# Turning queries and keys: six tokens in a row on each partition, two tokens per product, in all of the early attentions

## The chip, the cores and the metric

The kernel runs on one core of one Trainium2 chip. The metric is the time of one execution on the device in microseconds (us). Three runs of the kernel before took 796.45, 794.44 and 797.93 us; their median is 796.45 us.

## What is computed

Four batches of eight heads, 768 tokens, 64 numbers per head. Attention is local (tokens less than 16 apart) plus one summary per block of 32 tokens: the block's largest key in each coordinate and its mean value. The heads side by side then form a 768 x 512 matrix per batch, which goes through a two-dimensional Fourier mix, a normalisation and a two-layer network. In short:

```
k_sum = k.reshape(B, H, nb, 32, D).max(axis=3);  v_sum = v.reshape(B, H, nb, 32, D).mean(axis=3)
scores = concat(where(|i-j| < 16, q k^T / 8, -1e9), q k_sum^T / 8 + log(32))
x = softmax(scores) @ concat(v, v_sum)          # heads side by side: (4, 768, 512)
u = x + real(fft over tokens of fft over columns of x)
out = u + relu(norm(u) @ w_ch1) @ w_ch2
```

All arithmetic is in float32; the weights arrive as 64-bit floats and are converted on the chip.

## The kernel before

The heads are worked in pairs: pair g holds heads 2g (e = 0) and 2g + 1 (e = 1), whose 64 coordinates fill 128 partitions. For the scores, queries and keys have to stand with the coordinates on the partitions and the tokens along the row (tiles `qt` and `kt`, 128 x 768). In memory they stand the other way, so each pair is loaded with tokens on partitions (`load`) and turned (`prepare`).

There are three ways of turning. Batch 0 (`is_wide`) loads three tokens in a row on each partition (768 bytes), half h of the tokens at a time. For every half, each of the three tokens and each of the two heads, TensorE multiplies the 128 x 64 block by the identity (line 718) and writes the result three columns apart into a bank of PSUM; the bank then stands in token order for both heads, and ScalarE copies it (128 x 384, line 719) into a contiguous piece of `kt` or `qt`. A tensor takes twelve such products and two copies. Batch 1, and pair 0 of batch 2, load two tokens in a row (512 bytes, three pieces j for each head) and turn the 128 x 128 block of both tokens in one product (line 725): six products a tensor. One product's result has the first token on partitions 0 to 63 and the second on 64 to 127, so four copies of 64 x 384 (line 727) write the columns two apart. All later pairs go through a transposition on VectorE (line 711); the change doesn't touch them.

The first attention (`first_attention`, batch 0) is laid down in the order of the program on TensorE and VectorE: nothing is moved there by a scheduler. For each pair: the scores of one half (line 748, products in which the two heads alternate; line 752, the scores of the block summaries, which need the key maxima of line 700), the exponentials on ScalarE (line 754), the multiplication by the mask on VectorE (line 571); then the second half; then `finish_pair` for the pair before (values, line 775), then `prepare` of the pair after next, then `sum_values` (line 765 on TensorE, line 767 as a copy). Pairs 0 and 1 are prepared ahead of this loop and within its first step. When the pairs are done, the Fourier mix of batch 0 starts (lines 1252 and 1256, with copies at 1257 and 1258), and the attention of batch 1 is woven in between by a driver that deals out steps; there line 791 are the scores, 814 and 816 the block sums and their scaling, 826 and 831 the values.

All loads named here go out on SP's queue, in program order while the first part runs. The PSUM banks of the turning come from a pool of four (`bank` in batch 0, `abank` later; in the latter the scores and the values of attention stand too). ScalarE takes its instructions in order, so copies, exponentials and conversions of weights (lines 1091 and 1104) queue behind each other.

Of the kernel before, what the change touches and what calls it, by code (L numbers as in the profile page):

```python
# [16 lines left out]
P = 128  # L17
# [471 lines left out]
def _main_program(ctx, tc, q, k, v, moe_w_ch1, moe_w_ch2, out):  # L489


    nc = tc.nc
    B, H, S, D = q.shape
    DM = H * D
    DF = moe_w_ch1.shape[1]
    NST = S // P
# [7 lines left out]
    S2 = S // 2  # L504
    F2 = S // 4
    HT = NST // 2
# [17 lines left out]
    ident = cpool.tile([P, P], FP, name="ident")  # L524
# [24 lines left out]
    def fetch(out, in_):  # L549

        ins = nc.sync.dma_start(out=out, in_=in_)
        if in_order[0]:
            tc.keep_in_program_order(ins)
        return ins.ins

    def abank(shape, name):
        return psum.tile(shape, FP, tag="attn", bufs=4, name=name)

    def bank(shape, name):
        return psum.tile(shape, FP, tag="bank", bufs=4, name=name)  # L560
# [16 lines left out]
    nat, marks = {}, {}  # L577

    def load(b, g, *which):

        for n in which or (1, 0):
            t = nat[b, g, n] = apool.tile([P, 2, NST // 2, 2 * D], FP, tag="nat", bufs=4, name=f"{'qk'[n]}n_{b}_{g}")
            if (b, g) > (2, 0):
                t = nat[b, g, n] = t.rearrange("p e j n -> p (e j n)").rearrange("p (m c) -> p m c", c=32)
                for e in range(2):
                    for h in range(2):
                        r, o = D * e + 32 * h, (q, k)[n][b, 2 * g + e].offset + 32 * h
                        fetch(out=t[r:r + 32], in_=bass.AP((q, k)[n].tensor, o, [[D, 32], [32 * D, S // 32], [1, 32]]))
                continue
            if is_wide(b):  # L590
                t = nat[b, g, n] = t.rearrange("p e j n -> p (e j n)").rearrange("p (e h s d) -> p e h s d", e=2, h=2, s=HT)
                fetch(out=t.rearrange("p e h s d -> p (e h) (s d)"),
                      in_=(q, k)[n][b, 2 * g:2 * g + 2].rearrange("e (h p s) d -> p (e h) (s d)", p=P, s=HT))
                continue
            fetch(out=t.rearrange("p e j n -> p (e j) n"),
                  in_=(q, k)[n][b, 2 * g:2 * g + 2].rearrange("e (j p s) d -> p (e j) (s d)", p=P, s=2))

# [59 lines left out]
    is_wide = lambda b: b == 0  # L659
# [39 lines left out]
    def key_maxima(g):  # L699
        nc.vector.tensor_reduce(out=km_bufs[g % 2][:, 0:nb], in_=kt_bufs[g % 2][:, W:W + S].rearrange("p (n f) -> p n f", f=BLOCK),  # L700
                                op=ALU.max, axis=AX.X)

    def prepare(b, g, *which):
        qn, kn = (nat[b, g, n] for n in range(2))
        kt = kt_bufs[g % 2]
        qt = apool.tile([P, S], FP, tag="qt", name=f"qt_{b}_{g}") if 0 in (which or (0,)) else None
        for n in which or (1, 0):
            src, dst = (kn, kt[:, W:W + S]) if n else (qn, qt)
            if (b, g) > (2, 0):
                with tc.issue_after(marks["dense"]):  # L710
                    nc.vector.transpose(out=dst, in_=src.rearrange("p m c -> p (m c)"))
                continue
            if is_wide(b):
                for h in range(2):
                    ps = bank([P, S2], f"qk_{b}_{g}_{h}")
                    for s in range(HT):
                        for e in range(2):
                            nc.tensor.matmul(ps[D * e:D * (e + 1), s:S2:HT], src[:, e, h, s, :], ident, start=True, stop=True)
                    nc.scalar.copy(out=dst[:, S2 * h:S2 * (h + 1)], in_=ps)
            else:  # L720
                for e in range(2):

                    ps = abank([P, S2], f"qk_{b}_{g}_{e}")
                    for j in range(NST // 2):
                        nc.tensor.transpose(ps[:, P * j:P * (j + 1)], src[:, e, j, :], ident)
                    for s in range(2):
                        nc.scalar.copy(out=dst[D * e:D * (e + 1), s:S:2], in_=ps[D * s:D * (s + 1)])  # L727
        if which == (0,):
            nat[b, g] = qt
            return  # L730
        if (b, g) != (1, 1):
            with tc.issue_after(marks["fold", 0]) if (b, g) == (1, 0) else ExitStack():
                key_maxima(g)
        nat[b, g] = qt
# [113 lines left out]
    def first_attention():  # L848
# [3 lines left out]
        wt["fold"] = split_fold(0, fold)  # L852
        p = {0: wide_scores(0, 0, lambda: add_blocks(0))}
        prepare(0, 1)
        sum_values(0, 0)
        load(0, 3)
        def finish_pair(g):
            wide_values(0, g, p[g], x)
# [9 lines left out]
        for g in range(NP - 1):  # L868
            p[g + 1] = wide_scores(0, g + 1, (None, lambda: add_blocks(1), finish_last_but_one)[g])
            if g < NP - 2:  # L870
                finish_pair(g)
                prepare(0, g + 2)
                sum_values(0, g + 1)
                for par in range(2):
                    fold_sequence(par, g)
            if g == NP - 3:
                load(1, 0)
                get_tables(0, lambda: load_raw(1))
                load_raw(2)
                sum_values(0, g + 2)  # L880
# [106 lines left out]
    def gen_attention(b):  # L987
# [3 lines left out]
        if b == 2:  # L991
            load(2, 1)
            load(2, 2)
# [7 lines left out]
        for g in range(NP + 1):  # L1001
# [44 lines left out]
            if n1:  # L1046
                prepare(*n1, *((1,) if b > 1 else ()))
# [432 lines left out]
    ps = bank([P, 512], "warm")  # L1480
# [18 lines left out]
    for vw in vw_bufs:  # L1499
        nc.gpsimd.tensor_copy(out=vw[:, :, D].rearrange("p (e n) -> p e n", e=2),  # L1500
                              in_=count[:, None, :].to_broadcast([P, 2, NQ]))
# [51 lines left out]
    for b in range(B):  # L1553
# [14 lines left out]
        if b == B - 2:  # L1568
# [9 lines left out]
            ps = bank([1, 1], "flag_ps")  # L1578
# [42 lines left out]
```

## Time and profile before

| what | value |
|---|---|
| median of three runs | 796.45 us |
| the profiled execution | 793.7 us |
| its span on the page | 791.9 us |
| granted TensorE clock | 0.999 |
| TensorE busy | 776.3 us, 98% |
| VectorE busy | 492.0 us, 62% |
| ScalarE busy | 224.7 us, 28% |
| turning copies of batch 0 (line 719) | 16 of 128x384, 478 and 479 ns in the mean |
| turning copies of batch 1 and pair (2,0) (line 727) | 40 of 64x384, 507 and 508 ns in the mean |
| first attention | from about 5 us to 44 us of the span |

The page gives busy time by engine and the chain of work that ended last; PEld is TensorE's loading of the stationary operand, which overlaps the products. A timeline shows instructions in order of time, like ones merged; the bracket after a line gives the idle time before it and who ended it.

### The profile page before, as it was taken

To read this page: it belongs to the slowest core of one execution; us is meant where nothing else is said; L and a number is where in the kernel's file an instruction comes from. 1 tells how busy PE (TensorE), PEld (TensorE's weight loads), DVE (VectorE), ACT (ScalarE), POOL (GpSimd) and SP (SyncE) were. 2 spreads that over 40 slices of the span, in tenths; PEclk is the share of its full clock that TensorE was granted. 3 is DMA by queue.
4 is the path that set the end of the run, shared out by engine and by line. 5 is a ranking of instruction groups with operands and counts; after the bars stand their busy time and mean duration, and the time that the engine had idled before them with its cause. 6 is when DMAs were issued, how large, how long until landed. Compare 5 with 4: busy or idle time off the path is not lost.

```text
span 791.9 us, 14352 instructions
## 1 busy us (share of the span) xinstructions
PE 776.3 (98%) x5920; PEld 562.9 (71%) x5920; DVE 492.0 (62%) x1019; ACT 224.7 (28%) x491; POOL 47.9 (6%) x85
## 2 busy tenths in 40 slices
PE   8998999999999999999999999999999999999997
PEld 6777655445588866787578866788569875886686
DVE  5899988787988556752758544653677623533352
ACT  3564757226525022100236012200226111001200
POOL 0000000000000020200210020300120000000000
PEclk9999999999999999999999999999999999999999
DMA  9999787695956179976342169610614153106001
GB/s 212 189 262 246 190 268 190 210 284 201 240 186 152 46 206 263 218 110 184 137 153 94 54 208 211 183 55 11 243 37 140 54 215 134 51 0 233 0 28 56
DMA packets 133353, 121.82 MB, mean 154 GB/s; under 512 B 94464, under 2 KB 114912, under 8 KB 133088
## 3 DMA queue, kind: packets, MB, share of 16 engines
q1 hardware_dynamic: 132160, 118.53, 54.0%
q0 software_dynamic: 576, 2.10, 0.8%
q8 instruction: 48, 0.79, 0.4%
q10 hardware_dynamic: 544, 0.20, 0.1%
q14 instruction: 25, 0.20, 0.1%
HBM read 97.22 MB, written 23.59 MB: 153 GB/s over the span
## 4 chain that ended last, share of the span: by engine, by line
PE 88%; DVE 5%; ACT 4%; DMA 2%; issue 1%; DVEq 0%
PE hx L1368 19%; PE ox L1437 18%; PE hz L1368 9%; PE oz L1437 9%; PE hy L1368 5%; PE o L1414 5%; PE oy L1437 5%; PE y L1252 3%; PE sc L791 2%; PE mx L1211 2%; PE av L826 2%; PE unt L1342 1%; PE av L831 1%; DMA qn<-in_q_dram 1%; PE ss L808 1%; ACT kt L727 1%
## 5 line engine op out<-in xcount | busy, mean ns | idle before, releaser
L1368 PE MATMUL hx<-u,w 128*128 128x384 f32 x512 | 185.4, 491 | 2.4 <-ACT h L1385 1.0
L1368 PEld LDWEIGHTS hx<-u,w 128*128 128x128 f32 x512 | 95.2, 190 | 71.3 <-ACT p L797 3.8
L1368 PE MATMUL hz<-u,w 128*128 128x384 f32 x256 | 93.0, 486 | 0.0
L1437 PE MATMUL oz<-w,s 128*128 128x256 f32 x336 | 81.3, 380 | 0.0
L1437 PE MATMUL ox<-w,s 128*128 128x256 f32 x336 | 80.1, 380 | 0.0
L1437 PE MATMUL ox<-w,h 128*128 128x256 f32 x336 | 79.6, 381 | 0.0
L571 DVE TENSOR_TENSOR x<-ox,x 128x256 f32<-128x256 f32 x84 | 35.5, 422 | 66.2 <-PE ox L1437 65.9
L1368 PEld LDWEIGHTS hz<-u,w 128*128 128x128 f32 x256 | 48.6, 190 | 33.9
L1437 PEld LDWEIGHTS ox<-w,h 128*128 128x128 f32 x336 | 63.1, 190 | 10.8 <-issue 1.2
L1437 PEld LDWEIGHTS ox<-w,s 128*128 128x128 f32 x336 | 63.2, 190 | 9.1 <-DVE x L571 0.3
L1437 PEld LDWEIGHTS oz<-w,s 128*128 128x128 f32 x336 | 63.3, 190 | 8.9 <-DVE x L571 0.4
L1379 ACT COPY h<-hx 128x384 f32<-128x384 f32 x32 | 15.3, 477 | 191.6 <-PE hx L1368 191.5
L571 DVE TENSOR_TENSOR h<-hy,h 128x384 f32<-128x384 f32 x32 | 17.8, 557 | 48.9 <-PE hy L1368 48.8
L1368 PE MATMUL hy<-u,w 128*128 128x384 f32 x128 | 46.8, 487 | 0.0
L571 DVE TENSOR_TENSOR h<-hx,h 128x384 f32<-128x384 f32 x32 | 17.8, 556 | 45.2 <-PE hx L1368 44.0
L1414 PE MATMUL o<-w,h 128*128 128x512 f32 x96 | 42.2, 595 | 0.7 <-DVE w L571 0.7
L1398 ACT ACTIVATE h<-hx 128x384 f32<-128x384 f32 x32 | 15.7, 489 | 89.4 <-PE hx L1368 89.4
L1437 PE MATMUL oy<-w,h 128*128 128x256 f32 x168 | 40.1, 380 | 0.0
L571 DVE TENSOR_TENSOR x<-oz,x 128x256 f32<-128x256 f32 x42 | 17.8, 423 | 30.4 <-PE oz L1437 30.1
L1368 PEld LDWEIGHTS hy<-u,w 128*128 128x128 f32 x128 | 24.2, 190 | 17.1 <-DVE h L571 0.7
L1437 PEld LDWEIGHTS oy<-w,h 128*128 128x128 f32 x168 | 31.8, 190 | 4.4
L1414 PEld LDWEIGHTS o<-w,h 128*128 128x128 f32 x96 | 18.0, 190 | 23.6 <-issue 20.7
(166 smaller groups left out, 1072.5 us busy)
## 6 DMA issues: line engine op xcount, KB each, us to landing
w<-dw SPq DMA_DIRECT2D x44, 896.0 KB, 5.6
words<-in_moe_w_ch_dram SPq DMA_DIRECT2D x32, 512.0 KB, 5.8
dw<-w SPq DMA_DIRECT2D x12, 896.0 KB, 7.0
vw<-in_v_dram SPq DMA_DIRECT2D x47, 192.0 KB, 6.2
out_dram<-x SPq DMA_DIRECT2D x23, 256.0 KB, 2.0
vb<-in_v_dram SPq DMA_DIRECT2D x24, 192.0 KB, 7.2
kn<-in_k_dram SPq DMA_DIRECT2D x9, 384.0 KB, 6.3
qn<-in_q_dram SPq DMA_DIRECT2D x9, 384.0 KB, 6.9
```

Of the source, the lines that this page charges most:

```text
L571: return nc.vector.tensor_tensor(out=out, in0=in0, in1=in1, op=op).ins
L727: nc.scalar.copy(out=dst[D * e:D * (e + 1), s:S:2], in_=ps[D * s:D * (s + 1)])
L791: nc.tensor.matmul(ps[h][r:r + 64, i, :], kt[rows, o:o + 64], qt[rows, o:o + BLOCK], start=True, stop=True)
L808: nc.tensor.matmul(ps[r:r + 32, :], km[rows, :], qt[rows, S2 * h:S2 * (h + 1)], start=True, stop=True)
L826: nc.tensor.matmul(av[r][32 * j:32 * (j + 1), t, :], p[rows, h, i - NB2 * h, :], vw[rows, i, :], start=(t == 0), stop=False, skip_group_ch ...
L1211: nc.tensor.matmul(out, y[:, g], table, start=False, stop=True, skip_group_check=True)
L1252: nc.tensor.matmul(y, fgs[b][par][:, st, P * g:P * (g + 1)], fs[par][:, g % 2, st, :], start=(st == 0), stop=(st == n - 1))
L1368: ins = nc.tensor.matmul(ps, w[:, a, kk, :], u[:, r, kk, :], start=start and kk == 0, stop=stop and kk == 1, skip_group_check=True)
L1379: nc.scalar.copy(out=c11, in_=X)
L1398: nc.scalar.activation(out=c21, in_=X, func=AF.Relu)
L1414: nc.tensor.matmul(ps, h[:, n, hf, P * t:P * (t + 1)], wt[2, b, j][:, 2 * hf:2 * hf + 2, :], start=(n, hf) == (0, 0), stop=(n, hf) == (NC ...
L1437: nc.tensor.matmul(ps, left[a][:, n, :], wt[2, b, j][:, r, :], start=start and n == 0, stop=stop and n == NC - 1, skip_group_check=True)
```

## The change

`load` now takes one form for all pairs up to (2,0): six tokens in a row on each partition, 1536 bytes, 256 rows per tensor. Partition p holds tokens 6p to 6p + 5 of each head. `prepare` turns two of them at once in 128 x 128 products, three products a head, in batch 0 too. Product j gives the tokens 6p + 2j (partitions 0 to 63) and 6p + 2j + 1 (64 to 127) for all p. Four copies per tensor of 64 x 384 put them in token order: for a fixed j they write columns six apart, and the three j lie two columns from each other. The queries of the very first pair are copied by VectorE, all else by ScalarE. The order of the instructions on the engines and queues is otherwise the same.

```
-            if is_wide(b):
-                t = nat[b, g, n] = t.rearrange("p e j n -> p (e j n)").rearrange("p (e h s d) -> p e h s d", e=2, h=2, s=HT)
-                fetch(out=t.rearrange("p e h s d -> p (e h) (s d)"),
-                      in_=(q, k)[n][b, 2 * g:2 * g + 2].rearrange("e (h p s) d -> p (e h) (s d)", p=P, s=HT))
-                continue
-            fetch(out=t.rearrange("p e j n -> p (e j) n"),
-                  in_=(q, k)[n][b, 2 * g:2 * g + 2].rearrange("e (j p s) d -> p (e j) (s d)", p=P, s=2))
+            fetch(out=t.rearrange("p e j n -> p e (j n)"),
+                  in_=(q, k)[n][b, 2 * g:2 * g + 2].rearrange("e (p t) d -> p e (t d)", p=P))
...
-            if is_wide(b):
-                for h in range(2):
-                    ps = bank([P, S2], f"qk_{b}_{g}_{h}")
-                    for s in range(HT):
-                        for e in range(2):
-                            nc.tensor.matmul(ps[D * e:D * (e + 1), s:S2:HT], src[:, e, h, s, :], ident, start=True, stop=True)
-                    nc.scalar.copy(out=dst[:, S2 * h:S2 * (h + 1)], in_=ps)
-            else:
-                for e in range(2):
-
-                    ps = abank([P, S2], f"qk_{b}_{g}_{e}")
-                    for j in range(NST // 2):
-                        nc.tensor.transpose(ps[:, P * j:P * (j + 1)], src[:, e, j, :], ident)
-                    for s in range(2):
-                        nc.scalar.copy(out=dst[D * e:D * (e + 1), s:S:2], in_=ps[D * s:D * (s + 1)])
+            for e in range(2):
+
+                ps = (bank if is_wide(b) else abank)([P, S2], f"qk_{b}_{g}_{e}")
+                for j in range(NST // 2):
+                    nc.tensor.transpose(ps[:, P * j:P * (j + 1)], src[:, e, j, :], ident)
+                for s in range(2):
+                    copy = nc.vector.tensor_copy if (b, g, n) == (0, 0, 0) else nc.scalar.copy
+                    copy(out=dst[D * e:D * (e + 1)].rearrange("r (p j s) -> r j p s", p=P, s=2)[:, :, :, s],
+                         in_=ps[D * s:D * (s + 1)].rearrange("r (j p) -> r j p", p=P))
```

## The prediction

> **What bounds the kernel now.** I read the busy shares first, then the chain that ended last, then the timeline of the first 50 us, then the groups by shape.
>
> ```profile
> PE 776.3 (98%) x5920; PEld 562.9 (71%) x5920; DVE 492.0 (62%) x1019; ACT 224.7 (28%) x491; POOL 47.9 (6%) x85
> ...
> PE 88%; DVE 5%; ACT 4%; DMA 2%; issue 1%; DVEq 0%
> ```
>
> TensorE is busy 98% of the span and owns 88% of the chain. So 1 us in which TensorE has nothing to do is nearly 1 us of time, and ACT's 28% is an average that says nothing of the 30 us where the change sits. The timeline of the third head pair's turning (g = 2 of batch 0; columns: start, us, engine, line, operation, in brackets the idle time before it and who ended it):
>
> ```profile
> 21.59 1.35 PEld L718 LDWEIGHTS qk<-ident,kn 128*64 128x64 f32 x24
> ...
> 22.57 0.48 ACT L719 COPY kt<-qk 128x384 f32<-128x384 f32 x1 [1.39 <-PE qk L718]
> ...
> 22.86 1.40 PEld L718 LDWEIGHTS qk<-ident,qn 128*64 128x64 f32 x24
> ...
> 23.27 0.48 ACT L719 COPY kt<-qk 128x384 f32<-128x384 f32 x1 [0.23 <-PE qk L718]
> ...
> 23.93 1.08 ACT L719 COPY qt<-qk 128x384 f32<-128x384 f32 x2 [0.18 <-PE qk L718]
> ...
> 24.76 1.10 PEld L748 LDWEIGHTS sc<-qt,kt 64*96 64x96 f32 x24
> ```
>
> Products lead here and ACT waits for them. From the first product to the first score it is 24.76 - 21.59 = 3.17 us; keys take 22.86 - 21.59 = 1.27 us of products. The same view gives 30.74 to 34.13 = 3.39 us for pair 3. In pair 1 ACT is held by the exponentials until 12.93, its first key copy starts at 12.88, and scores start at 15.70: 2.82 us. In pair 0 products start at 5.13 and scores at 8.09. Batch 1 already turns two tokens at once; there ACT leads:
>
> ```profile
> 73.30 0.64 PEld L725 LDWEIGHTS qk<-ident,kn 128*128 128x128 f32 x6 [0.62 <-issue]
> ...
> 73.88 2.06 ACT L727 COPY kt<-qk 64x384 f32<-64x384 f32 x4
> 73.90 0.69 PEld L725 LDWEIGHTS qk<-ident,qn 128*128 128x128 f32 x6
> ...
> 75.96 2.11 ACT L727 COPY qt<-qk 64x384 f32<-64x384 f32 x4
> ...
> 77.04 0.82 PEld L826 LDWEIGHTS av<-vw,p 64*32 64x32 f32 x62 [0.44 <-ACT qt L727]
> ...
> 78.65 0.75 PEld L831 LDWEIGHTS av<-vs,p 64*128 64x128 f32 x12 [0.79 <-ACT vs L816]
> ```
>
> A tensor's products take 73.90 - 73.30 = 0.60 us, but its four copies 2.06 us (0.52 us from start to start), and TensorE twice waits on ACT.
>
> **What the Trainium skill says.** "SBUF — State Buffer", section "Door 1: The DMA port swizzle", says SBUF has 16-byte lines, that two hits per line are needed for full speed, and that each access to a new line pays; it names 4 fp32 as the free limit and gives no price. The copies now write fp32 two apart (8 bytes, two per line); the changed ones write six apart (24 bytes, a new line each). The trace of before has one large access of that kind, a DVE reduction reading 64 apart:
>
> ```profile
> L650 DVE TENSOR_REDUCE vbs<-vb 96x64 f32<-96x512 f32 x2 | 2.1, 1026 | 0.0
> ...
> L700 DVE TENSOR_REDUCE km<-kt 128x24 f32<-128x768 f32 x16 | 15.1, 942 | 7.9 <-ACT kt L719 5.8 <-ACT kt L727 2.1
> ```
>
> With 0.15 us fixed (the two-point fit of L700 and the 192-element reduction at L1576, 354 ns), that is (1026-150)/512 = 1.71 ns an element against (942-150)/768 = 1.03: a factor of 1.66. So the trace agrees for reads. No row has strided writes over 8 bytes. Second, "TensorE: Matmul & The Clock Gate", section "What's actually happening", says the clock halves after an idle window of about 3.4 us and comes back after one busy window. The trace before has no such idle stretch (clock 9 in all slices).
>
> **The change part by part.**
>
> *Products, batch 0.* Twelve per tensor become six: 1.27 us becomes 0.60 us. Eight tensors: 8 x 0.67 = 5.4 us of TensorE work removed. It is a gain only where copies don't follow; they do.
>
> *Copies, batch 0.* Two of 128x384 (0.478 us) per tensor become four of 64x384 with a new stride. All tokens are interleaved now, so the scores, which alternate the two heads, need all eight copies of a pair; before they started after the third of four. ACT's price: 512 elements take 583 ns (L1343) and 384 take 478 (L719), so 0.82 ns an element and 0.163 us fixed. Bounds: below, 0.39 us a copy (two exponentials of 128x384 are 0.87 us together, 0.385 apart); the nearest row, L727, says 0.52; above, twice the time an element, 0.163 + 384 x 1.64 = 0.79. (In pairs 2 and 3 the key copies also wait for one another on ACT's own counter, as L727's do; the 0.52 contains that.) I take the factor 1.66: 0.163 + 384 x 1.36 = 0.69, 0.70 from start to start. For DVE: 0.15 + 384 x 1.71 = 0.81, 0.74 apart (its neighbours start some 0.07 before the end of the last).
>
> - Pair 2: the first copy starts after three products, 0.30, and the same tail as now (0.98 - 6 x 0.106 = 0.34): 0.64 + 8 x 0.70 + 0.06 = 6.30, against 3.17: +3.1.
> - Pair 3: 6.30 against 3.39: +2.9.
> - Pair 1: 8 x 0.70 + 0.06 = 5.66 against 2.82: +2.8. Its query transfer, landing at 13.77, is hidden by the key copies.
> - Pair 0: queries go to DVE, beside the keys on ACT. Queries landed at 1.24 + 5.1 = 6.34; longer rows may bring that 0.2 forward (512 packets of 768 bytes at 36 ns are 1.15 us on 16 engines; a 4632-byte row's rate, 181 ns, would make 256 of 1536 bytes 0.96). First copy at 6.14 + 0.64 + 0.07 = 6.85, last ends 3 x 0.74 + 0.81 = 3.03 later: scores at 9.9 instead of 8.09: +1.8. Queued behind the DVE copies is the key maximum (0.95 us), needed only 1.1 us after the scores begin: hidden.
>
> Sum, batch 0: 10.6 us. Nothing in TensorE's hand-written order fills these gaps; the sum products at L765 (0.34 us) lie inside them already. L767 on ACT and the multiplications on DVE shift along. After 45 us TensorE is again without a gap (14.69 of 15 us busy from 45 to 60), so nothing later absorbs the delay.
>
> *Copies, batch 1 and pair (2,0).* The count stays at 40, each dearer by 0.70 - 0.52 = 0.18 us. Pair (1,1), shown above: eight copies stand before L816, for which TensorE waits: +1.4. Pair (1,2), from 84.74 on: products wait for key copies (0.38 and 0.34 us) and L814 for query copies (0.69): +1.4. Pair (1,0), six copies from 46.0, 1.1 us, of which the 0.32 us idle ahead of L1257 takes part: +0.7. The rest stand beside dense products: +0.6. Sum 4.1. If the writes cost nothing, zero.
>
> *Loads.* Half or a third of the packets, same issues in the same order on SP; POOL untouched. TensorE waits 0.4 us in all for q and k, so beyond pair 0 I count nothing; if that cover were gone it would be at most that 0.4. The clock gate: TensorE idles about 4.7 us in each of pairs 2 and 3, enough for a halved window (up to 1.7 us each of three pairs, 5 us); zero taken, kept for the upper end.
>
> Total +14.7 us. The profiled execution took 793.7 us (span 791.9 plus 1.8 around it): 808.4. The median of the runs shown is 796.45, 2.75 above: 811.2.
>
> **The rivals.**
> 1. Strided writes cost nothing (0.52 us a copy, as L727). For it: reads and writes may differ. Pairs: 8 x 0.52 = 4.16, so +1.7, +1.5, +1.4, and +0.8 for pair 0 (DVE 3 x 0.48 + 0.55): +5.4, batch 1 unchanged: 801.9.
> 2. Twice the time an element (0.80 apart): +3.9, +3.7, +3.6, +2.3 = 13.5, batch 1 4.1 x 0.28/0.18 = 6.4, and one clock window 1.7: 818.
> 3. Not slower: two copies overlap like the exponentials, 0.385 apart, on ACT between copies of one bank. Then the shorter products nearly pay for them: +0.6, +0.4, +0.4 for pairs 2, 3 and 1, +0.8 for pair 0 (DVE as in 1), together 2.2, less 0.3 for earlier landings: 798.3, no change that can be told. It decides below 0.47 us from start to start (24 copies x 0.09 above 0.385 would add 2.1). Against it: L727 is 0.52 apart even where no wait stands between.
> That the change isn't made as told is excluded: the built order shows x3 products and eight 64x3x128 copies a pair, four of them on DVE.
>
> **How the numbers follow.** The likeliest, 811.2: 0.47. Rival 1: 0.27. Rival 2: 0.14. Rival 3: 0.09. Something unseen that makes it faster: 0.03. Half a percent, 4.0 us, is about what a measurement of this kernel can tell from no change. Faster 0.03, same 0.12 (rival 3 and a cheap rival 1), slower 0.85. The range reaches from the cheap side of rival 1 to rival 2: 800 to 819.
>
> **What would show it.** Copies of 64x384 near 0.69 us on ACT and 0.8 on DVE; scores of pair 2 some 6.3 us after its first product, TensorE idle before them with ACT as releaser; products 0.60 us a tensor; L816 of pair (1,1) 1.4 us later after its first key copy. Wrong if the copies are at 0.52 or less, if the scores start before the eighth copy, or if TensorE's gap is filled.

## The result, and the profile after

The changed kernel takes 837.78 us (median of 6 runs, 836.47 to 843.85) against 795.67 us before (6 runs, 794.44 to 797.93): 42.1 us slower, a ratio of 1.0535 with a 95% interval from 1.0507 to 1.0564. The forecast had the direction, but not the size: 811.2 us, with 819 as the upper end. The profiled execution took 838.19 us, its span is 836.4 us. (For one kernel below, whose copies write side by side, the ratio leaves out the slowest four of 20 runs, as over 1.5% above its fastest.)

The page of the kernel after, busy shares, the granted clock by slices, and the chain that ended last:

```profile
PE 794.2 (95%) x5776; PEld 573.4 (69%) x5776; DVE 496.7 (59%) x1023; ACT 253.6 (30%) x503; POOL 47.8 (6%) x85
...
PEclk7769979999999999999999999999999999999999
...
PE 84%; ACT 7%; DVE 5%; DMA 2%; issue 1%; POOL 0%; SPq 0%; DVEq 0%; POOLq 0%
```

Two things are new. ACT's share of the chain went from 4% to 7%, roughly 27 us more (7% of 836.4 less 4% of 791.9, both shares rounded). And TensorE is busy for 17.9 us *more* than before although it has fewer instructions (5776 for 5920): the row PEclk, 9 in every slice before, shows 7, 7, 6 in the first three and a 7 in the sixth, of 20.9 us each. TensorE ran slower there.

The timeline of the third pair's turning, the same stretch that the prediction showed of before:

```profile
35.10 0.64 PEld L712 LDWEIGHTS qk<-ident,kn 128*128 128x128 f32 x6
...
35.69 3.40 ACT L715 COPY kt<-qk 64x384 f32<-64x384 f32 x4 [1.65 <-PE qk L712]
35.71 0.69 PEld L712 LDWEIGHTS qk<-ident,qn 128*128 128x128 f32 x6
...
39.12 3.38 ACT L715 COPY qt<-qk 64x384 f32<-64x384 f32 x4
...
40.87 0.58 PE L737 MATMUL sc<-qt,kt 64*96 64x64 f32 x2 [3.90 <-ACT qt L715]
...
42.55 2.18 PE L737 MATMUL sc<-qt,kt 64*96 64x64 f32 x22 [1.10 <-ACT qt L715]
44.66 1.49 PE L741 MATMUL sc<-qt,km 64*32 64x384 f32 x4
```

The products are as short as forecast (35.71 - 35.10 = 0.61 us a tensor), the copies follow one another without a gap, and all but one product of the scores wait for them: 42.55 - 35.10 = 7.45 us from the first product of the turning, against 3.17 before and 6.30 forecast. A copy is 0.86 us from start to start ((39.12 - 35.69) / 4). The last two lines show the second loss. Half a pair's scores are 12 products in the program, and the trace has two records for each (x24; the turning's products have one). Before, the same 24 records, and the four of the key maxima behind them, read:

```profile
24.77 1.24 PE L748 MATMUL sc<-qt,kt 64*96 64x64 f32 x24
...
25.93 0.84 PE L752 MATMUL sc<-qt,km 64*32 64x384 f32 x4
```

Now 22 of the 24 take 2.18 us instead of 1.24 for all, and the four 1.49 instead of 0.84. No wait in a bracket accounts for that.

The groups by shape give the copies (columns: count, busy us, mean ns, idle before and who ended it):

```profile
L715 ACT COPY kt<-qk 64x384 f32<-64x384 f32 x36 | 30.3, 843 | 6.3 <-PE qk L712 5.8
L715 ACT COPY qt<-qk 64x384 f32<-64x384 f32 x32 | 27.0, 845 | 0.6
L715 DVE COPY qt<-qk 64x384 f32<-64x384 f32 x4 | 3.3, 825 | 5.1 <-PE qk L712 5.0
```

Three stretches of the first 60 us, before and then after (columns: length, then busy us and instructions of PE, PEld, DVE, ACT and POOL, granted clock, DMA share, GB/s):

```profile
0.00:20.00 20.00, 17.90 (x216) 12.01 (x216) 10.37 (x26) 7.68 (x15) 1.86 (x8) 1.00 0.94 214
20.00:45.00 25.00, 23.77 (x420) 18.39 (x419) 21.42 (x44) 11.26 (x21) 0.28 (x2) 1.00 0.99 220
45.00:60.00 15.00, 14.69 (x85) 13.23 (x84) 13.80 (x27) 10.85 (x31) 0.00 (x0) 1.00 1.07 234
```

```profile
0.00:20.00 20.00, 15.71 (x84) 10.46 (x84) 9.91 (x26) 7.81 (x11) 1.87 (x8) 0.75 0.89 228
20.00:45.00 25.00, 15.81 (x152) 11.39 (x152) 8.07 (x13) 15.03 (x20) 0.00 (x0) 0.70 0.42 84
45.00:60.00 15.00, 9.99 (x110) 7.02 (x108) 9.78 (x17) 9.09 (x13) 0.00 (x0) 0.73 0.47 111
```

TensorE has work for only 15.81 of 25 us, and does it at 0.70 of its clock. The delay stage by stage, from the two timelines: values of the first attention end at 70.20 us instead of 42.81 (+27.4); the first inverse Fourier products of batch 1 start at 116.55 instead of 82.52 (+34.0); the first output products (L1403) at 167.84 instead of 131.77 (+36.1); the products at 249.60 stood at 204.48 (+45.1); the end is +44.5 (two profiled executions are compared here; the medians are 42.1 apart). So 27 us arise in batch 0, where 10.6 had been forecast, and 17 in batch 1 and pair (2,0), where 4.1 had.

### The profile page after: what moved, and what is told of

It reads as the page before. It is cut to its first block, busy times and chain, and to the rows that moved or that the text cites. A ratio compares the mean times of both kernels' runs of the same rounds, so it can differ in the third digit from the quotient of the medians.

```text
span 836.4 us, 14084 instructions
## 1 busy us (share of the span) xinstructions
PE 794.2 (95%) x5776; PEld 573.4 (69%) x5776; DVE 496.7 (59%) x1023; ACT 253.6 (30%) x503; POOL 47.8 (6%) x85
## 3 DMA queue, kind: packets, MB, share of 16 engines
q1 hardware_dynamic: 124992, 118.53, 50.3%
## 4 chain that ended last, share of the span: by engine, by line
PE 84%; ACT 7%; DVE 5%; DMA 2%; issue 1%; POOL 0%; SPq 0%; DVEq 0%; POOLq 0%
PE hx L1357 18%; PE ox L1426 17%; PE hz L1357 9%; PE oz L1426 9%; PE o L1403 5%; PE hy L1357 5%; PE oy L1426 4%; PE y L1241 3%; ACT kt L715 3%; ACT qt L715 3%; PE sc L780 2%; PE mx L1200 2%; PE sc L737 2%; DMA words<-in_moe_w_ch_dram 2%; PE unt L1331 1%; PE av L815 1%
## 5 line engine op out<-in xcount | busy, mean ns | idle before, releaser
L1368 ACT COPY h<-hx 128x384 f32<-128x384 f32 x32 | 15.3, 477 | 191.5 <-PE hx L1357 191.5
L1403 PE MATMUL o<-w,h 128*128 128x512 f32 x96 | 43.9, 615 | 3.4 <-DVE w L571 3.4
L1403 PEld LDWEIGHTS o<-w,h 128*128 128x128 f32 x96 | 18.6, 196 | 27.4 <-issue 22.5
L737 PE MATMUL sc<-qt,kt 64*96 64x64 f32 x192 | 18.8, 352 | 17.1 <-ACT qt L715 14.1
```

What stands on the lines that cost most here:

```text
L737: nc.tensor.matmul(ps[e][0:WK, n - n0, :], kt[rows, QB * n:QB * n + WK], qt[rows, QB * n:QB * (n + 1)], start=True, stop=True)
L1368: nc.scalar.copy(out=c11, in_=X)
L1403: nc.tensor.matmul(ps, h[:, n, hf, P * t:P * (t + 1)], wt[2, b, j][:, 2 * hf:2 * hf + 2, :], start=(n, hf) == (0, 0), stop=(n, hf) == (NC ...
```

## The experiments

My theory after the result: the copies cost twice the time an element because of the write step, and the pauses of TensorE that they make throw its clock to half speed, which costs about as much again. Rivals: the copies alone (with all that waits behind them on ACT); the reading of PSUM in steps or the longer rows of the loads; and a clock that is lower for a reason that has nothing to do with the pauses.

**1. Each half of the change alone.** The first kernel keeps the new turning for batch 0 only, the second for batch 1 and pair (2,0) only.

```
+            if is_wide(b):
+                fetch(out=t.rearrange("p e j n -> p e (j n)"),
+                      in_=(q, k)[n][b, 2 * g:2 * g + 2].rearrange("e (p t) d -> p e (t d)", p=P))
+                continue
+            fetch(out=t.rearrange("p e j n -> p (e j) n"),
+                  in_=(q, k)[n][b, 2 * g:2 * g + 2].rearrange("e (j p s) d -> p (e j) (s d)", p=P, s=2))
...
+                    nc.scalar.copy(out=dst[D * e:D * (e + 1), s:S:2], in_=ps[D * s:D * (s + 1)])
```

The diff is that of the first, against the kernel after; its last line is the copy of batch 1 as it was. The second has the old lines under `is_wide(b)` instead.

> Batch 0 as changed; batch 1 and pair (2,0) loaded and turned as before. Theory (each part delays TensorE where it stands): the changed kernel was 27.4 us behind when the first Fourier products began (74.01 against 46.62), so the time is about 796 + 27 = 823 us, the copies of batch 1 are back at 0.51 us and the clock is full from 75 us on. Rival (a late start makes everything after it late, the dearer copies of batch 1 cost little): above 832.

> Batch 0 as before; batch 1 and pair (2,0) loaded in rows of six tokens and copied six columns apart. Theory: the changed kernel lost 44.5 - 27.4 = 17 us after the first Fourier products began, with copies of 0.84 us ahead of the scaled sums and of the weights' conversion on ACT; so about 812 us. Rival (that loss came from the late start of the first attention): at most 800.

Batch 0 alone: 823.88 us, ratio 1.0344 (1.0299 to 1.0388), that is +28.1 us over its 795.78. Batch 1 alone: 809.53 us, 1.0184 (1.0143 to 1.0224), +13.75 us. Together 41.9, the whole is 42.1: the halves add, and each has to be explained by itself. One part of the first expectation failed: with the copies of batch 1 back at 0.51 us the clock is not full from 75 us on, but at half once more, from 108.1 to 111.5 us.

**2. What makes a copy dear.** Two kernels change only how the copy goes through its tokens. In the first it writes side by side (the tokens come out in another order, the same for keys and queries: that part of the computation is changed). In the second the order of the loop inside a copy is turned: it writes 8 bytes apart, as before the change, and reads PSUM 512 bytes apart instead.

```
-                    copy(out=dst[D * e:D * (e + 1)].rearrange("r (p j s) -> r j p s", p=P, s=2)[:, :, :, s],
-                         in_=ps[D * s:D * (s + 1)].rearrange("r (j p) -> r j p", p=P))
+                    copy(out=dst[D * e:D * (e + 1), S2 * s:S2 * (s + 1)], in_=ps[D * s:D * (s + 1)])
```

```
+                    copy(out=dst[D * e:D * (e + 1)].rearrange("r (p j s) -> r p j s", p=P, s=2)[:, :, :, s],
+                         in_=ps[D * s:D * (s + 1)].rearrange("r (j p) -> r p j", p=P))
```

> The changed kernel, but every copy writes its 384 columns side by side, so the tokens of keys and queries stand out of order (that part of the computation is changed). Number and size of the copies stay. Theory (the 24-byte step of the writes makes them dear): copies 0.48 to 0.52 us, time 800 to 808 us. Rival (64 rows or the shape with three pieces makes them dear): copies stay near 0.84 us, time 830 or more.

> The changed kernel, but each copy runs through the columns in token order: it writes 8 bytes apart and reads PSUM 512 bytes apart. Theory (a new line of SBUF at each write is what costs, PSUM reads are free): copies near 0.51 us, 800 to 808 us. Rival (any step over a line costs, on either side): copies 0.8 us or more, 830 us or more.

The groups of the first kernel, writes side by side:

```profile
L715 ACT COPY kt<-qk 64x384 f32<-64x384 f32 x36 | 17.0, 473 | 6.9 <-PE qk L712 6.3
...
L715 DVE COPY qt<-qk 64x384 f32<-64x384 f32 x4 | 2.2, 555 | 4.8 <-PE qk L712 4.7
```

The same groups of the second, writes 8 bytes apart and reads 512 apart:

```profile
L715 ACT COPY kt<-qk 64x384 f32<-64x384 f32 x36 | 18.1, 504 | 7.0 <-PE qk L712 6.5
...
L715 DVE COPY qt<-qk 64x384 f32<-64x384 f32 x4 | 2.2, 556 | 5.0 <-PE qk L712 4.9
```

The copies of line 727 in the kernel before tell the two steps apart on ACT, for they write 8 bytes apart too, but read PSUM in sequence:

```profile
L727 ACT COPY kt<-qk 64x384 f32<-64x384 f32 x20 | 10.1, 507 | 0.5 <-PE qk L725 0.3
```

So reading PSUM in steps of 512 bytes costs neither engine anything that can be told (ACT 504 ns against 507, DVE 556 against 555). Writing 8 bytes apart costs ACT some 30 ns (504 against 473), and it is the write step of 24 bytes that takes it from 504 to 843 ns. The times: 802.72 us (795.1 to 812.5 over 20 runs; ratio 1.0057, 1.0032 to 1.0082) and 809.07 us (1.0169, 1.0101 to 1.0238), the second a little over the 808 that had been expected at most. Neither is explained by its copies alone, for the second has copies like those of L727 before, and is still 13 us slower than the kernel before. The 20 runs of the first show why, since they are the same instructions every time:

| mean granted clock of the run | runs | time, us |
|---|---|---|
| 1.000 | 3 | 795.1 to 795.9 |
| 0.997 | 4 | 797.3 to 797.9 |
| 0.993 to 0.994 | 3 | 798.5 to 802.1 |
| 0.986 to 0.990 | 6 | 803.3 to 806.2 |
| 0.976 to 0.982 | 4 | 808.9 to 812.5 |

With short copies *and* a full clock the new turning costs about 1 us at most (795.1 to 795.9; the two runs of the kernel before that had a clock of 1.000 in the same rounds took 794.15 and 794.74, its median is 795.78). Everything above that goes with the clock; that the clock is the cause is for the next experiment to show.

A third kernel varies the step itself: batch 0 as before, and in batch 1 and pair (2,0) the copies write 12, 16, 32, 24 and 48 bytes apart, pair by pair (tokens again in another order, a changed part of the computation; queries go to DVE).

```
+                    step = {(1, 0): 3, (1, 1): 4, (1, 2): 8, (1, 3): 6, (2, 0): 12}[b, g]
+                    copy(out=dst[D * e:D * (e + 1), S2 * s:S2 * (s + 1)].rearrange("r (p f) -> r f p", f=step),
+                         in_=ps[D * s:D * (s + 1)].rearrange("r (f p) -> r f p", f=step))
```

> A look at single durations only; batch 0 is as before. In batch 1 and pair (2,0), turned two tokens at once, the copies of 64x384 read PSUM in sequence and write with a step that differs by pair: 12 bytes in pair (1,0), 16 in (1,1), 32 in (1,2), 24 in (1,3), 48 in (2,0); keys on ACT, queries on DVE. Tokens come out in another order, the same for keys and queries, so this part of the computation is changed. Known: side by side ACT 0.473 and DVE 0.555 us, 8 bytes apart 0.50 and 0.556, 24 bytes apart 0.842 and 0.825. If the price is set by how many writes fall into one line of 16 bytes (two are free, one is not), 12 bytes lies between (three of four writes alone in a line: some 0.70 us), and 16, 24, 32 and 48 bytes all give 0.84. If it grows with the distance, 16 bytes is below 0.84 and 48 above it.

The key copies of pairs (1,0), (1,1), (1,2), (1,3) and (2,0), one row for each pair's stretch of time (columns: shortest/median/longest ns, first and last start):

```profile
L729 ACT COPY kt<-qk x4: 681/688/707, 46.1 to 48.3; 64x384 f32<-64x384 f32 x4
...
L729 ACT COPY kt<-qk x4: 826/840/860, 74.9 to 77.5; 64x384 f32<-64x384 f32 x4
...
L729 ACT COPY kt<-qk x4: 862/862/882, 88.6 to 91.3; 64x384 f32<-64x384 f32 x4
...
L729 ACT COPY kt<-qk x4: 828/856/883, 126.6 to 129.7; 64x384 f32<-64x384 f32 x4
...
L729 ACT COPY kt<-qk x4: 827/831/859, 196.0 to 198.5; 64x384 f32<-64x384 f32 x4
```

At 12 bytes 0.69 us, from 16 bytes on 0.83 to 0.86, and no more at 48. DVE's are alike (0.68, then 0.84 to 0.85). That fits a price for each 16-byte line entered, and not one that grows with the distance: at 8 bytes, four writes enter two lines, at 12 bytes three, at 16 four; and 0.69 lies near the middle of 0.50 and 0.84.

**3. The clock, in batch 0.** Products of the identity with itself, into a PSUM bank that nothing reads, are put behind the turning of each pair of batch 0, where TensorE stands idle: 10, 20, 22 and 22 in the kernel after, 4, 10, 10 and 10 in the kernel of the turned copy loop. A third kernel shortens the pause instead: with the turned loop, DVE takes all queries of batch 0.

```
+            if is_wide(b) and n == 0:
+                ps = abank([P, P], "filler")
+                for _ in range((10, 20, 22, 22)[g]):
+                    nc.tensor.matmul(ps, ident, ident, start=True, stop=True)
```

```
-                    copy = nc.vector.tensor_copy if (b, g, n) == (0, 0, 0) else nc.scalar.copy
+                    copy = nc.vector.tensor_copy if (b, n) == (0, 0) else nc.scalar.copy
```

> The changed kernel with 10 to 22 products of the identity with itself behind the turning of each pair of batch 0, so that TensorE isn't idle while the copies run; they write a PSUM bank that nothing reads. Theory (idle stretches halve TensorE's clock, and that is the part of the loss which the copies' own length doesn't cover): granted clock 0.9 or more from 5 to 75 us, the scores of a pair's half at 1.2 us instead of 2.2, time 826 to 830 us. Rival (the clock has another cause, or the copies alone hold the path): 836 or more.

> As token_order, with 4 to 10 such products behind each pair's turning. Theory (of the 13 us that token_order loses, the copies' extra length is 5 and the clock the rest): 800 to 803 us, clock 0.95 or more in the first 60 us. Rival (the copies' count alone, or reading PSUM by steps): 807 or more.

> As token_order, with the queries of all pairs of batch 0 copied by DVE beside the keys on ACT. Theory (what holds TensorE is how long the eight copies take one after another): from a pair's first product to its scores 0.64 + 4 x 0.52 = 2.8 us against 3.2 to 3.4 us before, no idle stretch over 3 us, 792 to 798 us. Rival (DVE, with 32 us of work in the first 45, becomes late): 800 or more.

The same stretches as above, the kernel after with filling products:

```profile
0.00:20.00 20.00, 17.83 (x145) 13.64 (x146) 10.92 (x27) 11.29 (x15) 1.86 (x8) 1.00 0.95 238
20.00:45.00 25.00, 23.37 (x315) 19.88 (x315) 13.73 (x26) 17.47 (x25) 0.00 (x0) 1.00 0.49 103
45.00:60.00 15.00, 14.45 (x196) 10.65 (x196) 12.24 (x26) 10.58 (x17) 0.28 (x2) 1.00 1.02 306
```

Work was added, none was taken away, the copies still last 848 ns, and the kernel takes 821.65 us (ratio 1.0331, 1.0296 to 1.0367) instead of 837.78: 16.1 us less, and less than the 826 to 830 expected. The clock is at 1.00 in these stretches; it still falls to half in batch 1, from 90.8 to 101.1 and from 220.5 to 223.9 us. When the Fourier mix starts, 14.3 of the 16.1 us are there (59.74 instead of 74.01 us); from about there on TensorE's order differs a little between the two kernels, so the last 2 us are not surely the clock's. The two sides agree in size: the clock of the kernel after is at half from 10.2 to 20.4, 23.8 to 34.0, 40.9 to 51.1 and 57.9 to 64.8 us, 37.6 us in which TensorE was busy for some 33; half of that is 16.6. With the turned loop and fewer filling products it is 799.37 us (1.0048, 1.0031 to 1.0065; 800 to 803 had been expected) instead of 809.07, and there TensorE's order is the same in both but for the filling products. This settles the rival of a clock that is low for another reason: keeping TensorE at work keeps it up.

The third kernel missed: 808.43 us (1.0178, 1.0133 to 1.0223), where 792 to 798 had been expected. Its fourth pair shows why:

```profile
35.89 0.64 PEld L712 LDWEIGHTS qk<-ident,kn 128*128 128x128 f32 x6
...
36.48 2.08 ACT L715 COPY kt<-qk 64x384 f32<-64x384 f32 x4 [1.21 <-PE qk L712]
...
36.82 1.02 DVE L571 TENSOR_TENSOR p<-p,wide 128x384 f32<-128x384 f32 x2
...
39.26 2.27 DVE L715 COPY qt<-qk 64x384 f32<-64x384 f32 x4
...
41.67 1.67 PE L737 MATMUL sc<-qt,kt 64*96 64x64 f32 x17 [0.60 <-DVE qt L715]
```

The query copies could have started at 37, but DVE first had to weight and normalize the pair before; they start at 39.26 and end at 41.5. The pause was only moved to another queue, and the clock is at half from 9.3 to 19.5 and from 40.0 to 50.3 us.

**4. Batch 1.** The first kernel gives batch 1 and pair (2,0) the long rows and the turned loop, with batch 0 as before. The next two keep the dear copies of batch 1 (the kernel of 809.53 us) and fill TensorE's pause in pair (1,1), first with 18 products in a bank of their own, then with 6 in the bank of the value sums that follow.

```
+            if (b, g, n) == (1, 1, 0):
+                ps = abank([P, P], "filler")
+                for _ in range(18):
+                    nc.tensor.matmul(ps, ident, ident, start=True, stop=True)
```

```
-        ps = abank([P, D], f"vs_{b}_{g}")
+        ps = abank([P, P], f"vs_{b}_{g}")
+        if (b, g) == (1, 0):
+            for _ in range(6):
+                nc.tensor.matmul(ps, ident, ident, start=True, stop=True)
+        ps = ps[:, 0:D]
```

> Batch 0 as before; batch 1 and pair (2,0) in rows of six tokens, copies in token order. Theory (batch 1 already had six products and four copies a tensor; its loss of 14 us is all from the 24-byte step): copies 0.51 us, 794 to 797 us, no difference from before. Rival (the longer rows or the other layout matter by themselves): 800 or more, or 792 or less.

> Batch 1 and pair (2,0) alone changed, as in the run that gave 809.5 us (its copies are 0.85 us, its clock is at half for 10.2 us from 78.7 us on and for 3.4 us at 150 us). Added: 18 products of the identity with itself (about 0.10 us each) behind the query products of pair (1,1), into a PSUM bank that nothing reads, where TensorE stands idle waiting for copies anyway. If the clock carries the larger part of batch 1's 13.8 us, the slices from 75 to 105 us show clock 1.00, TensorE reaches the first inverse Fourier products some 3 to 4 us earlier and the time is 804 to 807 us (6.8 to 10 us of half clock, of which TensorE worked most). If instead the length of the copies and what ACT does late (conversion of the weights) carries it, the clock is full but the time stays within 1 us of 809.5. The rival of my prediction that has copies at twice the time an element and no clock effect in batch 1 gives 796.5 + 6.4 = 803 us with or without the added products.

> Batch 1 and pair (2,0) alone changed, as in the run at 809.5 us, and again identity products to hold the clock, now only six (0.23 us each, 1.4 us), in the bank of the value sums of pair (1,0) just before these overwrite it: they lie in the 1.3 us in which TensorE waited from 77.3 to 78.6 us, take no other bank, and end before the products that follow can start. The planner shifts a few products of the next pair, as in the run with 36 of them. If the half clock from 78.7 us on is worth time, the slices from 75 to 90 us are at clock 1.00 and the products of values and the inverse Fourier transform after it (17 us of half clock and waiting) end some 3 us earlier: 805 to 808 us. If it is worth nothing, because TensorE stands behind ACT there at any clock, the time stays at 809 to 811 us with the clock at 1.00.

The first: 795.58 us, ratio 0.9998 (0.9985 to 1.0011), with copies of 507 and 508 ns. Rows of 1536 bytes, PSUM reads in steps and 8-byte writes together cost batch 1 nothing, and gain nothing. All of its 13.75 us hangs on the write step.

The second missed: 812.81 us (1.0211, 1.0180 to 1.0242) where 804 to 807 had been expected. Each of these products is two of the trace's records, 0.23 us and not the 0.10 that I had assumed; they ran from 76.8 to 81.1 us, took the bank that the value sums were waiting for, and these came 4 us late. It tells nothing of the clock.

The third fits into the pause. Stretches of the kernel without filling products, then of this one (columns as above):

```profile
75.00:80.00 5.00, 2.71 (x46) 2.11 (x44) 4.62 (x21) 4.92 (x7) 0.00 (x0) 0.87 0.53 176
80.00:85.00 5.00, 3.91 (x78) 3.44 (x79) 1.48 (x3) 4.95 (x9) 0.00 (x0) 0.50 0.01 3
85.00:90.00 5.00, 5.00 (x108) 4.30 (x106) 4.62 (x5) 2.06 (x5) 0.00 (x0) 0.61 0.02 6
```

```profile
75.00:80.00 5.00, 3.04 (x26) 2.55 (x24) 4.62 (x21) 4.92 (x7) 0.00 (x0) 1.00 0.49 159
80.00:85.00 5.00, 3.67 (x126) 3.21 (x126) 1.46 (x3) 4.95 (x9) 0.00 (x0) 1.00 0.02 3
85.00:90.00 5.00, 4.57 (x114) 2.81 (x114) 5.00 (x6) 4.04 (x7) 0.00 (x0) 1.00 0.20 70
```

805.97 us (1.0135, 1.0111 to 1.0158) against 809.53: 3.6 us less, though the two ratios' intervals overlap, and from 100 us on TensorE's order is no longer the same in the two kernels. The first inverse Fourier products, just behind this stretch, start at 86.42 instead of 89.37, 2.95 us earlier, which is the surer number. (Before it was 82.52.) So in this pause the clock carries about 3 us. It is not the clock's whole part in batch 1, for this kernel still has two stretches at half speed (3.4 us each, at 94.9 and 204.1 us). Without filling products TensorE is busy for 12.4 of the 13.7 us at half speed, and half of that is 6.2. By this estimate the clock carries from 3 to 6 of the 13.75 us, and some 8 to 11 are left to the copies and what they hold up.

Part of these arises where the trace of the kernel after shows it. ACT and DVE in pair (1,3)'s turning, and the wait of TensorE that follows:

```profile
163.53 3.47 ACT L715 COPY kt<-qk 64x384 f32<-64x384 f32 x4
167.02 1.74 ACT L715 COPY qt<-qk 64x384 f32<-64x384 f32 x2
...
169.09 1.69 ACT L715 COPY qt<-qk 64x384 f32<-64x384 f32 x2
...
171.22 1.15 ACT L1080 ACTIVATE words<-words,rebias 128x1024 int32<-128x1024 int32 x1
```

```profile
172.40 1.23 DVE L1095 SCALAR_TENSOR_TENSOR words<-words 128x1024 int32<-128x1024 int32 x1 [2.74 <-ACT words L1080]
```

```profile
PE o L1403 <- DVE w L571: 3.4, 1, 3.4
```

```profile
PE o L1414 <- DVE w L571: 0.7, 1, 0.7
```

The four fences are ACT, DVE, the list of TensorE's waits from 165 to 190 us (columns: waited for, us in total, times, longest), and the same wait before the change. The conversion of the expert weights has a step on ACT (L1080). It stands in ACT's queue behind the eight copies, comes late, DVE waits for it, and the output products wait 3.4 us for the weights (0.7 us before). Nothing of the turning is read here: the pair's own scores come far later. Behind pair (2,0) TensorE waits again for a copy on ACT (L1368), which stands behind that pair's copies and the next conversion:

```profile
235.81 1.56 PE L1357 MATMUL hx<-u,w 128*128 128x384 f32 x4 [1.93 <-ACT h L1368]
```

Before, the same wait is 0.23 us. Both waits are in the kernel with batch 1 alone as well (3.4 and 1.9 us), and in the one with the turned loop in batch 1 the first is back at 0.75 us. A third wait for L1368, 2.3 us up to 249.60, is not one of these: ACT had stood idle for 3.2 us ahead of that conversion, whose weights had only just landed, and with batch 1 alone it is 0.36 us.

## Why the prediction was wrong

**What held.** Copies bound the turning, not products; products came to 0.61 us a tensor (0.60 forecast); the pauses stand where they were forecast, with ACT as the releaser; the longer loads cost nothing that can be told (795.58 us with them in batch 1; 795.1 to 795.9 at a full clock with them everywhere); TensorE's 0.4 us wait for queries is gone; the key maximum behind DVE's copies is hidden. The scaled sums of pair (1,1) came later by more than forecast: 6.95 us after the first key copy with batch 1 alone (82.06 - 75.11) against 4.20 before (78.08 - 73.88), 2.75 us and not 1.4. Scores before the eighth copy had been named as a sign of being wrong, and strictly it came: the first product of a half goes after the sixth copy (40.87, two records), the other 11 wait for the eighth (42.55). It changes nothing in the sum.

**The term that was mis-sized: a copy.** I took 1.66, DVE's factor for reads 256 bytes apart, and got 0.69 us on ACT. It is 0.84 on ACT, (843 - 163) / 384 = 1.77 ns an element against 0.82: a factor of 2.2, at and slightly above the upper bound (0.79) that I had named; 0.825 on DVE against 0.81. What misled me was the factor. DVE's price for an element, 1.71 ns, taken over as it stands, gives 0.163 + 384 x 1.71 = 0.82 us for ACT too, and (825 - 150) / 384 = 1.76 ns is what DVE's own copies cost: with a line for each write the two engines pay alike, though ACT is faster on rows written side by side (473 ns against 555). The page of the Trainium skill that I cited, "SBUF — State Buffer", section "Door 1: The DMA port swizzle", with its 16-byte lines and two hits for each, was the better guide: from 16 bytes on each write pays for a line of its own, whatever the distance. Its free limit of 4 fp32, read as a step, does not hold here: fp32 written 4 apart (16 bytes) cost 0.84 us a copy, 2 apart 0.50. In the sum this is 8 x (0.856 - 0.70) = 1.25 us for each of three pairs and 0.6 in pair 0 (scores at 10.54, forecast 9.9): 10.6 becomes 15.0 for batch 0. Measured with the clock held up, it is 13.1 (the first Fourier products start at 59.74 with filling products, 46.62 before). Had I taken it, the forecast would have stood about where rival 2 stood, 818, still 20 us short.

**The step that failed: the clock gate, "zero taken", 5 us for the upper end.** It is 14 to 16 us in batch 0 and 3 to 6 in batch 1. No reason stood beside the zero. I had the rule in hand, and applied it in two wrong ways. First, I looked for windows without any work, and found pauses of 4.7 us that would hold one at most. Second, I charged one window for each (1.7 us). The Trainium skill, "TensorE: Matmul & The Clock Gate", section "What's actually happening", says one idle window of about 3.4 us halves the clock and one busy window restores it. The unit is right: each of the 25 stretches at half speed in eight traces (the kernel after and seven of the experiments; the stretch at the very end of every trace left out) is a multiple of 3.41 us. But here a window need not be idle to halve it, and the stretches of batch 0 in the kernel after last three windows or two (10.2, 10.2, 10.2 and 6.8 us). I worked out TensorE's busy share of each window in the first 300 us of these traces (ends of products are modelled, so to a few hundredths):

| busy share of a window at full clock | next at half clock, these eight traces | the other five traces |
|---|---|---|
| below 0.46 | 14 of 14 | 6 of 7 |
| 0.46 to 0.70 | 11 of 27 | 1 of 10 |
| over 0.70 | 0 of some 590 | 0 of some 400 |

In the eight traces every stretch at half speed ended with a window that was at least 95% busy, often only with the second such window. A pair that pauses for 4 us and then has 15 us of work pays for all of that at half speed until such a window has passed. It also feeds itself: at half speed the pair's work takes longer, and the next pause finds the clock just back.

**The cover that failed: "The rest stand beside dense products: +0.6."** I counted who waits for the copies, and not who stands behind them on ACT. For pairs (1,3) and (2,0) that is the conversion of the weights (L1080) and the copy at L1368: in the kernel with batch 1 alone the delay against before grows from 8.9 us at the first output products to 13.2 at the end of that block (2.7 us more of waiting for the weights, and the 1.7 us of half clock behind that wait), and to 16.0 just behind pair (2,0). The other pairs, at 0.335 us more a copy instead of 0.18 and with 3 us of clock, make up the rest: +1.2 us up to pair (1,0), +5.6 to the end of (1,1), +2.1 in (1,2), where 0.7, 1.4 and 1.4 had been forecast.

**The rivals.** Rival 1, short copies, has its answer in the side-by-side kernel, which is at most about 1 us slower than before as long as the clock is full; above that its time goes with the clock. Rival 2 was nearest, with its copy price about right (0.80 forecast, 0.856 from start to start), and one window of clock where there were eleven in batch 0. Rival 3 fails on its own point: copies of 64x384 don't overlap, at 473 ns (four side by side take 1.97 us) as little as at 843.

## What to carry to other kernels

Price a strided write by the 16-byte lines that it enters: on both engines here two fp32 to a line cost what a dense copy costs (to within some 30 ns), one to a line costs 0.27 to 0.37 us more in 384 elements, and turning the loop so that the step falls on PSUM's side took ACT's copies from 843 to 504 ns. When a change makes TensorE wait, look at its busy share by windows of 3.4 us: in these traces the clock halved after 32 of the 58 windows below 0.70 and after none above, and then everything after the pause, not the pause alone, gets dearer. And for an instruction that grows on a shared engine, list what is queued behind it, up to the next time that this engine runs idle, not only who reads its result.

## What the runs showed that was not expected

Useless products made a kernel faster: 74 of them, 148 records on TensorE, took 16.1 us off (837.78 to 821.65). I could have been warned, for the kernel has such products in two places, before the change and after it: two at its start (line 1482, bank `warm`), and three behind the values of batch 0's last pair (`keep_busy`, lines 564 and 883; lines of the kernel before), all into banks that nothing reads. What these two are worth was not measured. The same instructions, with writes side by side, gave times that go with the mean clock, from 795.1 us at 1.000 upwards. That it depends on where the clock's windows fall on the pauses is argued, since only one run of a kernel leaves a trace. That they fall elsewhere in each execution can be seen: in the six traces of kernels that are alike up to 46 us (the one before, and those that change batch 1 alone), the grid of windows, drawn back to the start, begins 0.17, 1.66, 1.88, 2.15, 2.76 and 3.36 us after the first instruction. Reading PSUM 512 bytes apart costs neither engine anything that can be told (504 ns against 507 on ACT, 556 against 555 on DVE), while writing SBUF 16 or more bytes apart costs DVE half as much again (825).
